# A 7x7 circular convolution by partial Fourier transform: plane operations moved behind round 15's sums, a third buffer for first sums, and another order of issuers for the last writes

## The chip, the cores and the metric

One Trainium2 chip, of which the kernel uses one core. The metric is device time in microseconds for one execution; the runs of the kernel before took 256.21, 256.63 and 630.49 us, so their median is 256.63. In the profile the engines are called PE (TensorE matmul), PEld (TensorE weight load), DVE (VectorE), ACT (ScalarE), POOL (GpSimd) and SP (SyncE, which here only issues DMAs).

## The reference

An image of 224 x 224 pixels with 96 channels, x, is convolved with 7 x 7 taps of 96 x 96 weights, w. The reference goes through a two-dimensional Fourier transform, so the convolution is circular in both directions:

```python
def reference(x, w):                       # x 1x224x224x96, w 7x7x96x96, bf16
    wp = jnp.pad(w, ((0, H - K), (0, W - K), (0, 0), (0, 0)))
    Xf = rfft2(x.astype(float32), axes=(1, 2))
    Wf = rfft2(wp.astype(float32), axes=(0, 1))
    Yf = jnp.einsum('bhwi,hwio->bhwo', Xf, Wf)
    return irfft2(Yf, s=(H, W), axes=(1, 2)).astype(bfloat16)
```

## The kernel before

**Stages.** The kernel transforms only along the rows' direction H, in blocks of 28 rows (j, 8 of them), with 17 frequencies (rounds s = 0 to 16; 0 and 16 are real, the others complex). Along W it keeps the seven taps and folds them by a two-phase scheme into three small products per frequency (m = 0, 1, 2 in the code) on differences and sums of the pixels, the planes J. W is cut into 7 tiles of 32 pixels (t = 0 to 6; the last is called TL). Each tile goes through three steps. The forward transform fills xf (matmuls with Fm). Then come 17 rounds, one for each frequency, written to a scratch buffer in HBM (tiles 0 to 5) or kept on chip (tile 6). Then comes the inverse transform (matmuls with Gm, or with GY for the last tile), which reads the scratch buffer, and whose result is written to the output. The inverse work of the tile before and the forward work of the tile after are filled in between the matmuls of a round (`mid` and `end`). Tiles 0 and 1 run four rounds apart beside each other; from tile 2 on one tile follows another.

**A round** is the function b_round (line 578). It takes two PSUM banks, b0 and b1, out of eight that are handed round in turn. A complex round does this:

- TensorE: 19 matmuls of 96x96 into b0, then the fill, then 14 into b1.
- ScalarE copies three parts of b0 into tt_ (scaled by -0.5).
- VectorE forms the first sums u (line 667) out of the rest of b0 and tt_, which releases b0. After the fill it forms v (line 675 or 678) out of b1 and tt_, which releases b1.
- The y sum, v plus u into the buffer yf (or, in the last tile, xn and xf), is ysum (line 681). It runs on VectorE where `ydve` is set and on GpSimd elsewhere, and it is the last reader of u and v.

tt_, u and v come from one pool, tv, with two buffers for each name: the third round from a given one reuses its buffers and has to wait until that round's y sum has read them.

**Plane operations.** Three rounds share one plane buffer J. The function jit (line 518) returns three VectorE operations that fill it from xf: the four differences, one sum, and two sums of differences; a real round needs only the differences. From tile 2 on they are issued in bursts, a group ahead: the dictionary plan (line 951) says in which round. The next tile's first group is issued in round 14. In a burst round all three stand behind that round's v and y sum, and GpSimd's sums that follow in a round with plane operations are made to wait for the last of them (line 697).

**Order.** Every engine executes its instructions in the order in which the code issues them; each issue is tied to the one before (helper at line 92, so nearly all rows of the profile have that line, and the tiles' names tell them apart).

**The end.** After tile 6's rounds, its y sums are transposed by VectorE, and 16 pairs of matmuls make the output of the eight blocks, two halves for each block. VectorE and ScalarE empty one half each into a buffer, and then a DMA of 168 KB writes the block: blocks 0, 2, 4 and 6 from SyncE, 1, 3 and 5 from GpSimd, 7 from ScalarE (line 1005).

Of the kernel before, what the change touches and what calls it, by code (L numbers as in the profile page):

```python
# [9 lines left out]
F32 = mybir.dt.float32  # L10
ALU = mybir.AluOpType
# [9 lines left out]
NJ = 8  # L21
# [13 lines left out]
SA = 13  # L35
# [6 lines left out]
SH2 = (0, 8, 13, 17)  # L42
FR0 = (0, 8, 17)
FR2 = ((0, 10, 24, 10), (10, 17, 34, 6))
MERGE = ()
NP2 = 0
FI = 6
LROUND = {8: 16, 11: 15}
# [10 lines left out]
def kernel(  # L59
# [7 lines left out]
    _, H, W, C = x.shape  # L67
# [504 lines left out]
    def pairs(ap):  # L572
        return ap.rearrange("p (r g o) -> p g r o", r=2, o=2)

    def yp(ap):
        return ap.rearrange("p g (r o) -> p g r o", o=2)

    def b_round(t, s, mid, end, ydve=False, planes=()):
# [25 lines left out]
                TE.matmul(o, lhsT=pl[:, (HALO - k) * NJ:(HALO - k) * NJ + 128], rhs=wv,  # L604
                          start=(k == 0 and not add), stop=(k == len(tp) - 1 and not both and m != 2 or not add and not both and k == len(tp) - 1))
        b0, b1 = bank(), bank()
        merge = t < 2 and s in MERGE
        tt_ = tv_pool.tile([128, 4 * C], F32, name="tt_")
        if s in REAL and t == TL and s == NS - 1:
            mid()  # L610
            for part in range(2):
                conv(b1, part * 2 * C, 0, part, both=True)
                for mi, m in enumerate((2, 1)):
                    conv(b1, (part * 2 + mi) * C, m, part, add=True)
            SE.copy(out=yp(ym), in_=pairs(b1[:, 0:4 * C]))
            load["a"] += 480
            end()
        elif s in REAL:
            for part in range(2):
                conv(b0, part * C, 0, part)  # L620
            if t == TL:
                SE.copy(out=tt_.rearrange("p (r m o) -> p r m o", r=2, m=2),
                        in_=b0[:, 0:2 * C].rearrange("p (r o) -> p r o", o=C).unsqueeze(2).to_broadcast([128, 2, 2, C]))
            else:
                SE.copy(out=tt_[:, 0:2 * C], in_=b0[:, 0:2 * C])
            mid()
            settle(0)
            for mi, m in enumerate((2, 1)):
                for part in range(2):
                    conv(b1, (part * 2 + mi if t == TL else mi * 2 + part) * C, m, part)  # L630
            if t == TL:
                VE.tensor_tensor(out=yp(ym), in0=pairs(tt_[:]), in1=pairs(b1[:, 0:4 * C]), op=ALU.add)
            else:
                VE.tensor_tensor(out=ym,
                                 in0=tt_[:, 0:2 * C].rearrange("p (r o) -> p r o", o=C).unsqueeze(1).to_broadcast([128, 2, 2, C]),
                                 in1=b1[:, 0:4 * C].rearrange("p (m r o) -> p m r o", m=2, r=2), op=ALU.add)
            load["a"] += 110 + 0.9 * 192
            load["v"] += 540
            for f in planes:
                f()  # L640
            settle(1)
            end()
        else:
            v = tv_pool.tile([128, 2, 2, C], F32, name="v")
            if merge:
                conv(b0, 2 * C, 0, 0, both=True)
                conv(b0, 2 * C, 2, 0, add=True)
                conv(b0, 3 * C, 1, 0, add=True)
                conv(b0, 0, 0, 1)
                conv(b0, C, 0, 2)  # L650
                SE.mul(out=tt_[:], in_=b0[:, 0:4 * C], mul=-0.5)
                u, pr = tt_[:, 2 * C:4 * C].rearrange("p (m o) -> p m o", m=2), tt_[:, 0:2 * C]
            else:
                for part in range(3):
                    conv(b0, part * C, 0, part)
                conv(b0, 3 * C, 2, 0)
                conv(b0, 4 * C, 1, 0)
                u = tv_pool.tile([128, 2, C], F32, name="u")
                if t == TL:
                    SE.mul(out=tt_[:, 0:C], in_=b0[:, 0:C], mul=-0.5)  # L660
                    SE.copy(out=tt_[:, C:3 * C], in_=b0[:, C:3 * C])
                    load["a"] += 240
                else:
                    SE.mul(out=tt_[:, 0:3 * C], in_=b0[:, 0:3 * C], mul=-0.5)
                pr = tt_[:, C:3 * C]
            if not merge:
                VE.scalar_tensor_tensor(out=u[:], in0=b0[:, 3 * C:5 * C].rearrange("p (m o) -> p m o", m=2), scalar=-0.5,
                                        in1=tt_[:, 0:C].unsqueeze(1).to_broadcast([128, 2, C]), op0=ALU.mult, op1=ALU.add)
            mid()
            settle(0)  # L670
            for mi, m in enumerate((2, 1)):
                for pi, part in enumerate((1, 2)):
                    conv(b1, (pi * 2 + mi if t == TL else mi * 2 + pi) * C, m, part)
            if t == TL:
                VE.tensor_tensor(out=v[:], in0=pr.rearrange("p (r o) -> p r o", r=2).unsqueeze(2).to_broadcast([128, 2, 2, C]),
                                 in1=b1[:, 0:4 * C].rearrange("p (r m o) -> p r m o", r=2, m=2), op=ALU.add)
            else:
                VE.scalar_tensor_tensor(out=v.rearrange("p m r o -> p m (r o)"),
                                        in0=pr.unsqueeze(1).to_broadcast([128, 2, 2 * C]), scalar=-2.0,
                                        in1=b1[:, 0:4 * C].rearrange("p (m q) -> p m q", m=2), op0=ALU.mult, op1=ALU.add)  # L680
            def ysum(eng):
                if t == TL:
                    return eng.tensor_tensor(out=yp(ym), in0=pairs(v.rearrange("p r m o -> p (r m o)")),
                                             in1=u.rearrange("p m (g o) -> p (m g) o", o=2).unsqueeze(2).to_broadcast([128, C, 2, 2]), op=ALU.add)
                return eng.tensor_tensor(out=ym, in0=v[:],
                                         in1=u.unsqueeze(2).to_broadcast([128, 2, 2, C]), op=ALU.add)
            if ydve:
                ysum(VE)
            last = None
            for f in planes:  # L690
                last = f()
            settle(1)

            def pool_sum(after):
                y = ysum(GE)
                if after is not None:
                    tc.add_manual_dep(y.ins, after.ins.name, SYNC, reason="sum after VectorE")
            if (t, s) in YLATE:
                later.append((YLATE[(t, s)], pool_sum))
            elif not ydve:  # L700
                pool_sum(last)
            load["a"] += 490 if merge else 410
            load["v"] += (560 if ydve else 250 if t < 2 else 0) + (560 if merge else 900)
            end()
        if t != TL and s == y1 - 1:
            dma(scr_tiles[t].rearrange("w j s e -> (w j) s e")[:, y0:y1], yf[:, 0:y1 - y0].rearrange("p s r m o -> p s (r m o)"))
# [132 lines left out]
    stmp_cm.__exit__(None, None, None)  # L839
    yf_pool = ctx.enter_context(tc.tile_pool(name="yf", bufs=YBUF))  # L840
    tv_pool = ctx.enter_context(tc.tile_pool(name="tv", bufs=2))
    load["v"], load["a"] = BIAS, 0.0

    t_pool = t2_pool = yo_pool = None
# [87 lines left out]
    for t in range(2, NT):  # L932
# [16 lines left out]
        for g, (s0, s1) in enumerate(JGB):  # L949
            if g + 1 < len(JGB) - (t == TL) or t + 1 < NT:  # L950
                plan[s0 if g + 1 < len(JGB) else s0 - 1] = g
        for s in range(NS):
            now = ()
            if s in plan:
                g = plan[s]
                now = jit(t, g + 1) if g + 1 < len(JGB) else jit(t + 1, 0)
            if s == 3:
                queue_c(t - 1)
            if t in (3, 4):
                next(gp, None)  # L960
            mid = fills(qs, 2 * s)
            if t == TL and s in LROUND:
                now = late_planes(LROUND[s])
            if t == TL and SA - 1 <= s < NS - 1:
                now = [lambda i=s - SA + 1: turn_a(i)]
            b_round(t, s, mid, fills(qs, 2 * s + 1), s == SA - 1 if t == TL else bool(now), now)
    turn_b()
    load["v"] = 2 * BIAS + load["a"]
    for f in cj:
# [16 lines left out]
    def second(j, h, pc, yo):  # L986
# [3 lines left out]
        yj = yo[0:MO, (j % 2) * 2 * NC:(j % 2 + 1) * 2 * NC].rearrange("p (w h q) -> p h w q", w=4, h=2)  # L990
        tail_evac(yj[:, h], pc.rearrange("p (w q) -> p w q", w=4), NC)
    order = [(j, h) for j in range(NJ) for h in range(2)]
    warm(WARM0)
    live = {k: first(*k) for k in order[:FI]}
    LF = 4
    for i, (j, h) in enumerate(order):
        if i % 4 == 0:
            yo = t_pool.tile([128, TW // 2, 2 * C], BF16, name="tt").rearrange("p w e -> p (w e)")
        second(j, h, live[(j, h)], yo)
        k = i + 8 - LF  # L1000
        if FI <= k < len(order):
            live[order[k]] = first(*order[k])
        if i % 2 == 1:
            w0 = TL * 2 * TW
            eng = SE if j == NJ - 1 else GE if j % 2 else DE
            eng.dma_start(out=out[0, j * B:(j + 1) * B, w0:w0 + 2 * TW, :].rearrange("m (q w) c -> m q (w c)", q=4), in_=yo[0:MO, (j % 2) * 2 * NC:(j % 2 + 1) * 2 * NC])
    if not NP2:
        ps0_cm.__exit__(None, None, None)
# [30 lines left out]
```

## Time and profile before

| | us |
|---|---|
| median of three runs | 256.63 |
| the profiled execution | 255.99 |
| its span, first to last instruction | 254.28 |
| TensorE busy (matmuls) | 245.4 |
| VectorE busy | 214.8 |
| ScalarE busy | 200.4 |
| GpSimd busy | 107.9 |
| VectorE u waiting for GpSimd sums (yf, xn) | 5.3 and 1.2 |
| GpSimd sum, one (yf) | 1.00 |
| VectorE u, v | 0.35, 0.54 |
| last tile's transposes end, last matmuls begin | 243.6 |

The granted TensorE clock is 0.995 over the span. A matmul's time in the profile is its way through the array; since matmuls are pipelined, the next one starts 42 ns after a 96x96 one. A wait of TensorE is therefore best read from the distance between starts. The page's slices show TensorE at nine tenths or more in all but the first and the last slices, so waits inside the span are short and are found in the chain of waits, which lists in order of time which engine held up the end, and in the timelines of single engines. Landing of a DMA means that its last part has reported to its semaphore.

### The profile page before, as it was taken

What the parts mean: (1) busy time and instruction counts of PE and PEld (TensorE: products, weight loads), DVE (VectorE), ACT (ScalarE), POOL (GpSimd) and SP (SyncE); (2) the same over time, 40 slices, a digit from 0 to 9 for tenths busy, and PEclk for the clock granted to TensorE, in tenths of its full rate; (3) what the DMA queues carried; (4) which work ended last, traced back from release to release, by engine and by line L of the source; (5) the groups of instructions that cost most, each with busy time, mean ns of one, the idle gap of its engine ahead of it and who ended that gap; (6) DMA issues with size and microseconds to landing.
All of it is one profiled execution on the core that took longest, in us unless ns stands there. A gap on an engine that the chain in (4) does not pass through costs nothing.

```text
span 254.3 us, 11853 instructions
## 1 busy us (share of the span) xinstructions
PE 245.4 (97%) x4981; PEld 230.8 (91%) x4981; DVE 214.8 (84%) x463; ACT 200.4 (79%) x499; POOL 107.9 (42%) x173
## 2 busy tenths in 40 slices
PE   8999999999999999999999999999999999999990
PEld 2789999999999999999999989999999999999970
DVE  7999899899889979789688887788978889989981
ACT  7989977584966977998988879988897976567671
POOL 7886514454457444332433324533233332465430
PEclk9999999999999999999999999999999999999998
DMA  7953103711111589997959369697969853496245
GB/s 176 260 162 97 48 5 93 233 49 49 49 52 50 187 206 143 280 318 214 304 171 256 111 184 275 194 257 180 333 214 208 246 183 105 134 170 182 60 134 163
DMA packets 41511, 42.80 MB, mean 168 GB/s; under 512 B 30836, under 2 KB 33072, under 8 KB 41458
## 3 DMA queue, kind: packets, MB, share of 16 engines
q1 hardware_dynamic: 41140, 41.36, 59.0%
q8 instruction: 39, 0.64, 1.1%
q0 software_dynamic: 192, 0.52, 0.7%
q10 hardware_dynamic: 126, 0.17, 0.2%
q14 instruction: 14, 0.11, 0.2%
HBM read 22.37 MB, written 19.66 MB: 165 GB/s over the span
## 4 chain that ended last, share of the span: by engine, by line
PE 88%; DVE 3%; issue 2%; SPq 1%; DMA 1%; POOL 1%; ACT 1%; POOLq 0%; DVEq 0%
PE pb L92 88%; SPq L92 1%; DVE WF L92 1%; DMA out_dram<-J 1%; DVE J L92 1%; DVE u L92 1%; POOL yf L92 0%; POOL xf L92 0%; DVE v L92 0%; DVE xf L92 0%; POOLq L1034 0%; ACT xf L92 0%; DVE tt L92 0%; ACT tt__7303 L92 0%; ACT tt__574 L92 0%
## 5 line engine op out<-in xcount | busy, mean ns | idle before, releaser
L92 PE MATMUL pb<-WF,J 96*128 96x96 bf16 x2782 | 160.9, 206 | 0.1
L92 PEld LDWEIGHTS <-J 96*128 96x128 bf16 x2782 | 137.0, 98 | 7.1 <-issue 0.2
L92 POOL TENSOR_TENSOR yf<-v,u 128x384 bf16<-128x384 f32 x70 | 68.9, 1000 | 118.4 <-issue 63.9
L92 ACT CAST xf<-pb 96x408 bf16<-96x408 f32 (+8 forms) x146 | 68.3, 489 | 4.2 <-PE pb L92 2.2
L92 PE MATMUL pb<-WF,xf 96*128 96x96 bf16 x991 | 62.0, 206 | 0.9 <-ACT xf L92 0.4
L92 DVE TENSOR_TENSOR J<-xf 96x1824 bf16<-96x1824 bf16 (+1 forms) x82 | 56.2, 724 | 0.1
L92 PEld LDWEIGHTS <-xf 96*128 96x128 bf16 x991 | 49.3, 98 | 1.6 <-issue 0.7
L92 PE MATMUL pb<-Fm,xn 118*128 118x136 bf16 (+5 forms) x576 | 44.4, 203 | 0.2 <-DVE u L92 0.2
L92 PE MATMUL pb<-tt,Gm 102*84 102x384 bf16 (+1 forms) x132 | 32.1, 325 | 0.0
L92 ACT CAST WF<-pb 96x480 bf16<-96x480 f32 (+1 forms) x59 | 29.2, 570 | 0.6 <-PE pb L92 0.6
L92 ACT CAST yo<-pb 84x384 bf16<-84x384 f32 (+1 forms) x65 | 27.9, 485 | 2.3 <-PE pb L92 2.3
L92 PEld LDWEIGHTS <-xn 118*128 118x128 bf16 x576 | 29.0, 97 | 0.5 <-issue 0.3
L92 ACT CAST J<-pb 84x384 bf16<-84x384 f32 (+1 forms) x65 | 28.0, 486 | 0.9 <-PE pb L92 0.9
L92 DVE TENSOR_TENSOR J<-J 96x912 bf16<-96x912 bf16 (+2 forms) x41 | 22.5, 548 | 0.0
L92 PE MATMUL pb<-wq 128*128 128x120 bf16 (+1 forms) x288 | 21.8, 226 | 0.1
L92 PEld LDWEIGHTS <-wq 128*128 128x128 bf16 x288 | 19.7, 149 | 0.6 <-ACT wq L92 0.4
L92 POOL TENSOR_TENSOR xn<-v,u 128x384 bf16<-128x384 f32 x11 | 10.0, 923 | 8.7 <-DVE J L92 5.7
L92 DVE TENSOR_TENSOR yf<-v,u 128x384 bf16<-128x384 f32 x20 | 11.3, 567 | 0.8 <-DMA scr<-yf 0.2
L92 PEld LDWEIGHTS <-Gm 102*84 102x84 bf16 (+1 forms) x132 | 11.3, 118 | 0.1
L92 ACT COPY xf<-xf 96x816 bf16<-96x816 bf16 (+4 forms) x16 | 10.0, 683 | 0.0
L92 DVE TENSOR_TENSOR WF<-WF 96x960 bf16<-96x960 bf16 x14 | 9.4, 721 | 0.1
L92 PE MATMUL pb<-wu 128*128 128x512 bf16 x24 | 7.8, 504 | 1.1 <-DVE ct L92 1.1
(409 smaller groups left out, 254.5 us busy)
## 6 DMA issues: line engine op xcount, KB each, us to landing
scr<-yf SPq DMA_DIRECT2D x30, 288.0 KB
xn<-in_x_dram SPq DMA_DIRECT2D x12, 672.0 KB
tt<-scr SPq DMA_DIRECT2D x24, 336.0 KB
out_dram<-yo SPq DMA_DIRECT2D x12, 252.0 KB
out_dram<-J SPq DMA_DIRECT2D x12, 252.0 KB
tt<-scr SPq DMA_DIRECT2D x6, 288.0 KB
scr<-yf SPq DMA_DIRECT2D x6, 192.0 KB
WF<-in_x_dram SPq DMA_DIRECT2D x2, 343.0 KB
```

The source lines that it names most:

```text
L92: r = fn(*a, **k)
```

## The change

Three things. First, of the burst that prepares the next tile's first group (issued in round 14), only the four differences stay in round 14; the other two operations go to round 15, behind its v. Round 15's y sum stays on GpSimd and follows them. Second, u gets a pool of its own with three buffers; tt_ shrinks to three parts, and the last tile's real round 0 uses a v buffer for its copy. Third, the last writes are issued by SyncE (0, 1, 3, 5), GpSimd (2, 4, 6) and ScalarE (7). A branch that no round took (merge, with MERGE empty) is deleted. On every engine the order of instructions is as before, except that at four tile boundaries VectorE has the two plane operations behind u and v of round 15 in place of ahead of them.

```diff
-            tt_ = tv_pool.tile([128, 4 * C], F32, name="tt_")
+            tt_ = tv_pool.tile([128, 3 * C], F32, name="tt_")
...
             if t == TL:
-                SE.copy(out=tt_.rearrange("p (r m o) -> p r m o", r=2, m=2),
+                v = tv_pool.tile([128, 2, 2, C], F32, name="v")
+                SE.copy(out=v[:],
...
-                u = tv_pool.tile([128, 2, C], F32, name="u")
+            u = u_pool.tile([128, 2, C], F32, name="u")
...
     tv_pool = ctx.enter_context(tc.tile_pool(name="tv", bufs=2))
+    u_pool = ctx.enter_context(tc.tile_pool(name="u", bufs=3))
...
+        carry = []
         for s in range(NS):
-            now = ()
+            now, carry = carry, []
             if s in plan:
                 g = plan[s]
                 now = jit(t, g + 1) if g + 1 < len(JGB) else jit(t + 1, 0)
+                if g + 1 == len(JGB):
+                    now, carry = now[:1], now[1:]
...
-            b_round(t, s, mid, fills(qs, 2 * s + 1), s == SA - 1 if t == TL else bool(now), now)
+            b_round(t, s, mid, fills(qs, 2 * s + 1), s == SA - 1 if t == TL else s in plan, now)
...
+    WENG = (DE, DE, GE, DE, GE, DE, GE, SE)
...
-            eng = SE if j == NJ - 1 else GE if j % 2 else DE
+            eng = WENG[j]
```

More of the change, by code (lines that the diff above doesn't have):

```diff
@@ L44 @@
 FR2 = ((0, 10, 24, 10), (10, 17, 34, 6))
-MERGE = ()
 NP2 = 0
@@ L606, in b_round @@
         b0, b1 = bank(), bank()
-        merge = t < 2 and s in MERGE
-        tt_ = tv_pool.tile([128, 4 * C], F32, name="tt_")
+        tt_ = tv_pool.tile([128, 3 * C], F32, name="tt_")
         if s in REAL and t == TL and s == NS - 1:
@@ L631, in b_round @@
             if t == TL:
-                VE.tensor_tensor(out=yp(ym), in0=pairs(tt_[:]), in1=pairs(b1[:, 0:4 * C]), op=ALU.add)
+                VE.tensor_tensor(out=yp(ym), in0=pairs(v.rearrange("p r m o -> p (r m o)")), in1=pairs(b1[:, 0:4 * C]), op=ALU.add)
             else:
@@ L644, in b_round @@
             v = tv_pool.tile([128, 2, 2, C], F32, name="v")
[L645 to L652, printed above, removed]
-            else:
[L654 to L657, printed above, removed]
-                u = tv_pool.tile([128, 2, C], F32, name="u")
[L659 to L668, printed above, removed]
+            for part in range(3):
+                conv(b0, part * C, 0, part)
+            conv(b0, 3 * C, 2, 0)
+            conv(b0, 4 * C, 1, 0)
+            u = u_pool.tile([128, 2, C], F32, name="u")
+            if t == TL:
+                SE.mul(out=tt_[:, 0:C], in_=b0[:, 0:C], mul=-0.5)
+                SE.copy(out=tt_[:, C:3 * C], in_=b0[:, C:3 * C])
+                load["a"] += 240
+            else:
+                SE.mul(out=tt_[:, 0:3 * C], in_=b0[:, 0:3 * C], mul=-0.5)
+            pr = tt_[:, C:3 * C]
+            VE.scalar_tensor_tensor(out=u[:], in0=b0[:, 3 * C:5 * C].rearrange("p (m o) -> p m o", m=2), scalar=-0.5,
+                                    in1=tt_[:, 0:C].unsqueeze(1).to_broadcast([128, 2, C]), op0=ALU.mult, op1=ALU.add)
             mid()
@@ L701, in b_round @@
                 pool_sum(last)
-            load["a"] += 490 if merge else 410
-            load["v"] += (560 if ydve else 250 if t < 2 else 0) + (560 if merge else 900)
+            load["a"] += 410
+            load["v"] += (560 if ydve else 250 if t < 2 else 0) + 900
             end()
```

## The prediction

> **What bounds the kernel now.** The page's first part comes first, then the chain of waits in order of time, because a chain that is nearly all one engine shows by its few interruptions what can be won.
>
> ```profile
> PE 245.4 (97%) x4981; PEld 230.8 (91%) x4981; DVE 214.8 (84%) x463; ACT 200.4 (79%) x499; POOL 107.9 (42%) x173
> ```
>
> TensorE is busy 97% of 254.3 us. Busy could hide slow feeding, so I also took the distance between the starts of neighbouring matmuls: for 96x96 it is 42 ns in nearly all of 3765 cases, and all distances beyond the usual one of their shape add up to 6.3 us, 2.9 us of it in the first 30 us and 0.6 us in the last 12 us. Between lies what this change can win on TensorE. The chain in order of time (start, duration, what) names the places:
>
> ```profile
> 63.14 1.94 issue
> 65.08 1.02 POOL yf L92
> 66.10 0.02 issue
> 66.12 0.37 DVE u L92
> 66.49 0.04 issue
> 66.53 53.22 PE pb L92 x1186
> 119.75 0.04 DVEq L92
> 119.79 0.05 DVE u L92
> 119.83 0.04 issue
> 119.88 23.93 PE pb L92 x482
> ...
> 151.13 0.21 DVE u L92
> 151.33 0.04 issue
> 151.38 87.59 PE pb L92 x1778
> ```
>
> Three times in the middle TensorE waits for VectorE's u, the operation that empties bank b0 of a round. At 66 u itself waited for a GpSimd sum. At 119.8 and 151.3 the timeline of VectorE shows what stood ahead of u (last column: what ended an idle time, none here):
>
> ```profile
> 117.84 1.32 DVE L92 TENSOR_TENSOR J<-xf 96x1824 bf16<-96x1824 bf16 x2
> 119.09 0.47 DVE L92 TENSOR_TENSOR J<-J 96x608 bf16<-96x608 bf16 x1
> 119.47 0.35 DVE L92 SCALAR_TENSOR_TENSOR u<-pb,tt__3633 128x192 f32<-128x192 f32 x1
> 119.74 0.54 DVE L92 SCALAR_TENSOR_TENSOR v<-tt__3633,pb 128x384 f32<-128x384 f32 x1
> ```
>
> These are round 14's three plane operations (1.10, 0.31 and 0.47 us; the first line holds two) and round 15's u and v. ScalarE had u's other input ready at 118.05. The end is another stage:
>
> ```profile
> 244.69 4.42 SPq L92 DMA_DIRECT2D out_dram<-tt  x4
> 245.75 0.88 POOL L92 DMA_DIRECT2D out_dram<-tt  x1 [3.22 <-DVE tt L92]
> 246.85 0.59 POOL L92 DMA_DIRECT2D out_dram<-tt  x1 [0.23 <-issue]
> 248.15 0.59 POOL L92 DMA_DIRECT2D out_dram<-tt  x1 [0.70 <-ACT tt L92]
> 248.74 1.44 ACTq L92 DMA_DIRECT2D out_dram<-tt  x1
> ```
>
> The eight last writes are issued here. By the trace's landing records write 6 (SyncE) is complete at 253.02 and write 7 (ScalarE) at 253.19; then only the closing barrier runs.
>
> **Plane operations behind round 15's sums.** Four boundaries (tiles 2 to 5) move the 0.31 and 0.47 us operations from before u to behind v. Nothing is added; VectorE's work between round 14's y sum and round 16's stays the same. At 119.5 u can start when the first plane operation lets it, 117.84 + 1.02 = 118.86 in place of 119.47, and ends at 119.2. TensorE was ready at 119.57 (42 ns after its last start, 119.53) and started at 119.88, so this wait of 0.30 us goes. At 150.87 the same step brings u's end from 151.32 to 150.71, TensorE was ready at 150.91 and started at 151.38: 0.46 us go, and with v also 0.6 us earlier the 0.13 us that TensorE waits at 151.67 for v's bank. The boundaries at 182 and 214 show no TensorE wait, so they win nothing. Sum: 0.89 us.
>
> What the moved operations may delay: round 16's y sum follows them at 120.3 in place of 120.2, and its bank is next written by round 1, after 121.6. Round 15's GpSimd sum now has to wait for the last of them: v ends near 119.6, the operations near 120.3, and the sum started at 120.42 before, so it moves by nothing. The planes themselves are read in round 1 of the next tile (from 121.17), 0.9 us after they are done. All of that is costed at nothing; a slip of more than 0.9 us would uncover it.
>
> **Third buffer for u.** u of a round no longer waits for the GpSimd sum two rounds back but for the one three back; v keeps two buffers and takes over the wait for two back, which u held for it until now. So v can never wait longer than u did. VectorE waited so 15 times (5.3 us for yf, 1.2 us for the last tile's xn), but only at 66 did TensorE wait behind it: u starts at 65.68 (v's end) in place of 66.12 and ends at 66.04, ahead of TensorE's readiness at 66.22, so 0.31 us go. ScalarE is packed there (64.1 to 68), so it is what is late next; bounds 0 and 0.31, and I take 0.31 because no TensorE wait on ScalarE appears between 40 and 240.
>
> In the last tile the four waits of 0.31 us are on VectorE's own chain, which sets the end (u at 240.74, v, a GpSimd sum, the transposes). One would count 4 x 0.27 = 1.1 us there. The trace says no: a plane operation that starts while GpSimd sums is stretched. The 96x1824 one takes 1.10 us as a rule and 1.39 us at 62.70 and at 50.71, where GpSimd's sum ran 0.43 us into it; with 0.12 us of overlap (220.83, 225.51) it still takes 1.10. So it ends no earlier than the sum's end plus 0.97. In the last tile each of these operations already starts 0.11 to 0.12 us before a sum ends (225.51 against 225.63), and u coming 0.3 us earlier only makes it start that much deeper into the sum. I take 0; the other bound is 0.27, since v at 230.11 waits for TensorE and only the one wait after it (233.3) could carry to the end.
>
> The ScalarE copy of the last tile's round 0 goes into a v buffer, waiting for round 14's VectorE sum and an earlier GpSimd sum, both over 2 us old by then: nothing.
>
> **Last writes.** The halves of write k are ready at 244.66, 245.16, 245.81, 246.47, 247.13, 247.79, 248.28 and 248.66. SyncE issues 0.03 us after readiness and takes 0.80 to 0.93; GpSimd starts 0.36 to 0.59 after and takes 0.59 to 0.88. So write 1 goes out on SyncE at 245.65 when write 0's issue is over (was 245.75), 2 on GpSimd near 246.3 (245.84), 3 on SyncE at 246.5 (246.85), 4 on GpSimd near 247.5 (247.16), 5 on SyncE at 247.82 (248.15), 6 on GpSimd near 248.65 (248.31), 7 on ScalarE at 248.74 as before. From issue to landing the eight took 2.82, 2.87, 3.25, 3.57, 3.58, 4.15, 4.71 and 4.45 us: it grows with what is under way, not with the engine. Write 6 would land at 252.8 (4.15) to 253.35 (4.7). Write 7's issue took 1.44 us while SyncE and GpSimd issued beside it; SyncE is idle then after the change, so it costs between 0.8 and 1.44, and it lands between 252.6 and 253.2. The end moves from 253.19 to between 252.6 and 253.35: a win of 0.6 to a loss of 0.16. I take a win of 0.2, the middle.
>
> Sum: 0.89 + 0.31 + 0 + 0.2 = 1.4 us. The profiled execution took 255.99 (span 254.28 and 1.71 around it), so 254.6 on its scale. The two near runs are 256.21 and 256.63, and the stated median, 256.63, is 0.64 above the profiled one; the mean of the three, 256.28, less 1.4 gives 254.9.
>
> **Rivals.** *GpSimd is the worse issuer for the end.* For: it starts 0.36 us after readiness where SyncE takes 0.03, and write 6, next to last, now pays that. Against: GpSimd's landings lie on one line with SyncE's. Priced by the 0.3 us later issue alone: the 0.2 us become a loss of 0.2, total 1.0, 255.3. The Trainium skill, in DMA: Bandwidth & Descriptors, Latency and other measured facts, gives about 1 us to the first byte of a GpSimd DMA and 0.6 us for SyncE or ScalarE; by that estimate write 6 alone loses 0.4 us. Its section Issuing engines are not separate DMA queues adds that spreading issues over engines saves only issue time, since all run on the same 16 DMA engines; by that alone the end term is nothing and the total 1.2 us.
>
> *The waits come back elsewhere.* TensorE meets a bank that ScalarE empties late, at 66 and after the boundaries, as ScalarE is 79% busy. Then only the wait at 150.9 is won: 0.4 to 0.6 us, 255.8. Against it speaks that after 66 no TensorE wait other than these appears in 170 us.
>
> *Slower: the planes are late for round 1.* If the moved operations slip by over 0.9 us (their first in-queue chance is behind v, which needs TensorE's b1 and now GpSimd's sum), the next tile's first round stalls, four times. Past that point each 0.1 us costs 0.4; a slip of 1.4 us costs 2.0, less 1.4 won: 256.9. Against: v starts at 119.1 to 119.2 there and GpSimd is idle before it (3.14 us).
>
> *VectorE's relief counts too and the writes win their best*: 0.89 + 0.31 + 0.27 + 0.6 = 2.1, 254.2. *The change does nothing* because v takes over every wait: it would hold for the third buffer alone, and the boundary order is plain in the program, so it is only part of the second rival.
>
> **How the numbers follow.** Chances: forecast 0.52, GpSimd 0.18, waits back 0.16, slower 0.06, best 0.08. Predicted 254.9. The lower end takes in the best case on the profiled run's scale (255.99 - 2.1 = 253.9), the upper end a win of nothing on the median's (256.6); only the slower case is out, so the range 253.9 to 256.6 leaves under 2 in 10. Two per cent, 5.1 us, is about what a measurement of this kernel can tell from no change; every case lies inside: faster 0.02, same 0.95, slower 0.03, the tails for what I did not see.
>
> **What would show it.** In the changed profile no TensorE wait on u near 66, 119 and 151, u of round 15 right behind the first plane operation, v with the GpSimd waits, last landing at 252.6 to 253.4 less 1.2, and the 96x1824 operations of the last tile longer than 1.10 us. Wrong would be: new TensorE waits after 66 or in round 1, VectorE's transposes ending over 1.5 us earlier than before (243.6), or write 6 landing alone at the end.

## The result and the profile after

| | before | after |
|---|---|---|
| median (7 runs each) | 256.42 us | 255.59 us |
| range | 256.06 to 256.63, and one execution of 630.49 | 255.14 to 255.85 |
| ratio, 95% interval | | 0.9961, 0.9948 to 0.9974 |
| profiled execution | 255.99 | 255.59 |
| its span | 254.28 | 253.87 |
| last transpose ends, last write landed | 243.60, 253.19 | 243.11, 252.79 |

The change makes the kernel 0.8 us faster by the medians (0.3%) and 1.0 us by the ratio (0.4%), where 1.4 us were forecast. The spans differ by only 0.41 us, for two reasons that have nothing to do with the change. The two executions did not start alike: the matmul at 16 us, which no part of the change reaches, comes 0.21 us later in the execution after. And TensorE pauses there for 0.22 us at 173 us. Such differences of the first 16 us were 0 to 0.77 us among the executions below, with the profiled one of before the luckiest. So I compare the two traces matmul by matmul: both kernels have the same 4981 matmuls in the same order, and each step in the difference of their starts is a wait that came or went. A negative number is a wait that is gone.

| place (us in the trace before) | step, us | what it is |
|---|---|---|
| 60.5 | +0.11 | new wait for VectorE's weight difference WF |
| 66.5 | -0.32 | u near 66 us, which waited for a GpSimd sum |
| 119.9 | -0.30 | u of round 15 |
| 151.4 and 151.8 | -0.46 and -0.13 | u, then v of round 15 |
| 156.9 | +0.07 | new wait for a bank that ScalarE empties |
| 173 | +0.22 | pause without a cause in the trace; in this execution alone |
| 242.5 | +0.18 | longer wait of the first matmul with GY for the transposes |

The first part of the page, once more with TensorE at 97%, shows nothing of this:

```profile
PE 245.1 (97%) x4981; PEld 230.5 (91%) x4981; DVE 216.6 (85%) x463; ACT 200.3 (79%) x499; POOL 108.9 (43%) x173
```

The chain of waits does (start, duration, what; start and end of its part after 60 us):

```profile
60.71 0.00 issue
60.72 111.77 PE pb L91 x2364
172.49 0.06 issue
172.54 66.35 PE pb L91 x1352
...
242.57 0.55 DVE xf L91
243.12 0.04 issue
243.16 3.96 PE pb L91 x36
```

The chain no longer leaves TensorE for u at 66, 119.8 and 151.3: it stays there from 60.72 to 238.9 but for a 0.06 us step at 172.5. At the end it is on VectorE, as before. VectorE's timeline at the first boundary (start, duration, operation, in brackets what ended an idle time, none here) shows the new order:

```profile
117.75 1.09 DVE L91 TENSOR_TENSOR J<-xf 96x1824 bf16<-96x1824 bf16 x1
118.77 0.35 DVE L91 SCALAR_TENSOR_TENSOR u<-pb,tt__3634 128x192 f32<-128x192 f32 x1
119.03 0.54 DVE L91 SCALAR_TENSOR_TENSOR v<-tt__3634,pb 128x384 f32<-128x384 f32 x1
119.50 0.30 DVE L91 TENSOR_TENSOR J<-xf 96x304 bf16<-96x304 bf16 x1
119.72 0.46 DVE L91 TENSOR_TENSOR J<-J 96x608 bf16<-96x608 bf16 x1
120.11 0.54 DVE L91 TENSOR_TENSOR yf<-tt__3684,pb 128x384 bf16<-128x384 f32 x1
```

u starts at 118.77, right behind the first plane operation, and the other two follow v and are done by 120.2, before round 1 reads them.

The last writes (start of the issue, its duration; four of SyncE in one line):

```profile
244.20 3.93 SPq L91 DMA_DIRECT2D out_dram<-tt  x4
245.78 0.88 POOL L91 DMA_DIRECT2D out_dram<-tt  x1 [3.75 <-DVE tt L91]
247.02 0.59 POOL L91 DMA_DIRECT2D out_dram<-tt  x1 [0.36 <-ACT tt L91]
248.25 1.44 ACTq L91 DMA_DIRECT2D out_dram<-tt  x1
248.32 0.58 POOL L91 DMA_DIRECT2D out_dram<-tt  x1 [0.70 <-DVE tt L91]
```

ScalarE's issue takes 1.44 us as before, though SyncE is now done at 248.13 and idle. By the landing records write 7 lands last, at 252.79, and GpSimd's write 6 at 252.42.

### The profile page after: what moved, and what is told of

The parts are those of the page before. It is cut to its first block, busy times and chain, and to the rows that moved or that the text cites. A ratio compares the mean times of both kernels' runs of the same rounds, so it can differ in the third digit from the quotient of the medians.

```text
span 253.9 us, 11837 instructions
## 1 busy us (share of the span) xinstructions
PE 245.1 (97%) x4981; PEld 230.5 (91%) x4981; DVE 216.6 (85%) x463; ACT 200.3 (79%) x499; POOL 108.9 (43%) x173
## 4 chain that ended last, share of the span: by engine, by line
PE 91%; DVE 3%; ACT 2%; issue 1%; POOL 0%; POOLq 0%; DVEq 0%
PE pb L91 91%; ACT WF L91 1%; DVE WF L91 1%; ACT xf L91 1%; DVE J L91 1%; DVE v L91 1%; DVE u L91 0%; POOL xf L91 0%; DVE xf L91 0%; POOLq L1028 0%; DVE tt L91 0%; ACT tt__577 L91 0%; DVE wu L91 0%; DVE ct L91 0%; DVEq L91 0%
## 5 line engine op out<-in xcount | busy, mean ns | idle before, releaser
L91 POOL TENSOR_TENSOR yf<-v,u 128x384 bf16<-128x384 f32 x70 | 69.6, 1009 | 117.2 <-DVE v L91 61.2
```

The lines of the kernel that those rows point to most:

```text
L91: r = fn(*a, **k)
```

## The experiments

All ratios are to the kernel before, run on the same chip in the same session; a median of before stands beside them. "Shift to 239" is the step of the matmul starts between 40 and 239 us, against the profiled execution before, which leaves the unlike starts out. "GY wait" is how much later than usual the second matmul with GY starts (0.24 us before).

**The moved plane operations alone.** The kernel before, with the edit of jit's results only:

```diff
+        carry = []
...
-            now = ()
+            now, carry = carry, []
...
+                if g + 1 == len(JGB):
+                    now, carry = now[:1], now[1:]
...
```

> The kernel before with the moved plane operations alone. If the boundary waits are the main win (the forecast): TensorE's waits at 119.5 (0.30 us), 150.9 (0.46) and 151.7 (0.13) are gone, the one at 66.2 (0.31) stays, and the time falls by 0.5 to 0.9 us (ratio about 0.997). If the waits only come back elsewhere: new TensorE waits of the same size within a tile after each boundary, and a time within 0.3 us of the kernel before. If the planes come late: TensorE waits in round 1 of tiles 3 to 6, and a longer time.

Median 255.86 (before 256.71), ratio 0.998, 0.9955 to 1.0004; of itself the ratio leaves open whether there is a gain. The trace does not: shift to 239 is -0.79, in the steps -0.30, -0.46, -0.13 and +0.07 of the table. The wait at 66 stays; here in the chain, u and TensorE behind it:

```profile
66.92 0.37 DVE u L92
67.29 0.04 issue
67.34 171.62 PE pb L92 x3593
```

**The third buffer alone**, with the smaller tt_ that makes room for it; order of the plane operations and issuers as before:

```diff
-        tt_ = tv_pool.tile([128, 4 * C], F32, name="tt_")
+        tt_ = tv_pool.tile([128, 3 * C], F32, name="tt_")
...
-                u = tv_pool.tile([128, 2, C], F32, name="u")
+            u = u_pool.tile([128, 2, C], F32, name="u")
...
```

> The kernel before with the three-part tt_ and three buffers for u alone. If u's wait on GpSimd is what TensorE waited for at 66: that wait (0.31 us) is gone and the time falls by 0.1 to 0.3 us; the waits at 119.5 and 150.9 stay. If an early u only leads the next two-input VectorE operation into a GpSimd sum: the weight difference near 59 takes 1.4 to 1.5 us in place of 1.17, the 608-element operations of the last tile 0.70 in place of 0.466, TensorE's wait at 60.5 grows by 0.1, and of the 0.3 us only 0.2 is left. If the relief in the last tile counts after all: the transposes end over 0.6 us earlier.

Median 256.60, ratio 0.9994, 0.9986 to 1.0003. Shift to 239 is -0.24 (the steps at 60.5 and 66.5), and the GY wait rises to 0.43, which gives 0.19 back: 0.05 us remain. Of the three cases the second came: the weight difference takes 1.49 us, the 96x608 operations of the last tile 0.70. The chain shows the waits that this part leaves alone, and none at 66:

```profile
61.06 58.92 PE pb L91 x1299
119.98 0.04 DVEq L91
120.01 0.05 DVE u L91
...
151.35 0.21 DVE u L91
151.56 0.04 issue
151.60 88.19 PE pb L91 x1788
```

**The issuers alone.**

```diff
+    WENG = (DE, DE, GE, DE, GE, DE, GE, SE)
...
-            eng = SE if j == NJ - 1 else GE if j % 2 else DE
+            eng = WENG[j]
```

> The kernel before with the new issuers of the last writes alone. If the order of issuers is worth something (the forecast's 0.2 us): from the first write's readiness to the last landing 8.3 us in place of 8.53. If it is worth nothing, because the last issue is the same 1.44 us one on ScalarE: 8.5 to 8.65 us, and the time within 0.15 us of the kernel before. If GpSimd is the worse issuer: write 6 lands last and the stretch takes 8.7 us or more.

Median 256.70, ratio 0.9998, 0.9989 to 1.0006. From the first write's readiness to the last landing it takes 8.76 us; with the old issuers 8.53 (before) and 8.90 twice (the two runs above). That is none of the three cases: the stretch is longer than the profiled one before, yet write 7 lands last and not write 6, and the profiled one before turns out to be the shortest of three. A gain, if there is one, is too small for these times to show.

**The changed kernel again**, in the same session, unaltered.

> The changed kernel, unchanged. If the TensorE wait of 0.22 us at 172.3 without a semaphore, the one of 0.07 at 155.7, the VectorE pause of 0.29 us at 234.6 and the 0.21 us lost before 16 belong to that execution alone, they are absent or elsewhere here and the span is up to 0.5 us shorter (253.4); if they belong to the program, they come again at the same places and the span is 253.9.

Median 255.75, ratio 0.9965, 0.9953 to 0.9976. Shift to 239 is -1.06. The pause at 173 is absent; the new waits at 60.5 and 156.9 and the GY wait (0.42) recur. The parts add up to about that: 0.79 and 0.24.

**Write 7 on SyncE instead of ScalarE.**

```diff
-    WENG = (DE, DE, GE, DE, GE, DE, GE, SE)
+    WENG = (DE, DE, GE, DE, GE, DE, GE, DE)
```

> The changed kernel with write 7 issued by SyncE instead of ScalarE; all else as changed. In the changed kernel write 7 was ready at 248.17, ScalarE's issue of it took 1.44 us, and it landed last at 252.79, 0.37 us behind write 6. Theory: the long issue holds the end. SyncE takes 0.80 for the same write, so write 7's issue ends 0.64 us sooner, its landing comes 0.3 to 0.6 us sooner, and the time from the first write's readiness to the last landing falls from 8.6 to 8.7 to 8.2 to 8.4; ratio to the kernel before near 0.995, against 0.9961 of the change. Rival: the landings go one behind the other at the pace of the transfers, the backlog sets the end; then the issue takes 0.80 but the last landing does not move by over 0.1 us, and the ratio stays at 0.996 to 0.997.

Median 255.66 (before 256.58), ratio 0.9964, 0.9951 to 0.9978. The five issues of SyncE now are

```profile
244.06 4.84 SPq L91 DMA_DIRECT2D out_dram<-tt  x5
```

and write 7's takes 0.80 us where ScalarE took 1.44. Yet it lands at 252.60, 8.57 us after the first readiness, against 8.51 to 8.76 with ScalarE. The rival holds: the long issue costs nothing that these runs show.

**Moved operations and these issuers, u with two buffers.** The first experiment's kernel with the last writes of the one just told.

> The kernel before with the moved plane operations and with the new issuers, write 7 on SyncE; u keeps two buffers in the old pool. Theory: the third buffer's 0.2 us on TensorE are given back in the last tile (first GY matmul waits 0.42 us with it, 0.23 without), so leaving it out costs nothing: the same ratio as the three parts together with write 7 on SyncE, within 0.0008, TensorE 0.79 us earlier by 239 us (wait of 0.33 at 66.9 stays) and the first GY matmul's wait 0.22 to 0.24. Rival: the third buffer is worth its 0.24 us or more; then this one is 0.001 or more slower than that kernel.

Median 255.68, ratio 0.9966, 0.9953 to 0.9978: the same time without the third buffer as with it. At 239 us TensorE is 0.30 us behind the other kernel, but the GY wait is 0.22 and not 0.42, so at the end 0.09 us are left of it. The theory holds: what the third buffer wins near 66 us is given back in the last tile.

**The sums of the last tile left out.**

```diff
-                y = ysum(GE)
+                y = GE.memset(ym, 0.0) if t == TL else ysum(GE)
```

> The changed kernel, with the last tile's GpSimd y sums left out: a memset of the same output stands in the place of each sum (so those y values are not computed), with its waits on VectorE unchanged. Theory: a plane operation with two inputs in SBUF is held while a GpSimd operation reads SBUF; a memset reads none. So the 96x608 operations at 228.2 and 233.3 fall from 0.70 to about 0.47 us and the 96x1824 ones that begin inside a sum back to 1.10, u and v follow that much earlier. If VectorE's pause of 0.29 us between u and v near 234.6 comes from the same cause it goes too and the first GY matmul's wait falls from 0.42 to about 0.2. Rival: the operations are long because of their own waits or of TensorE; then they stay at 0.70 with the memset in place of the sum. If the pause stays, it is not GpSimd's reading that makes it.

One execution, 255.29 us. The 96x608 operations fall from 0.71 and 0.70 to 0.47 and 0.46 us, VectorE's pause is gone, and the first matmuls with GY run without a wait at all. But a memset reads neither u nor v and does not wait for them, so the memsets do not lie where the sums lay. It shows that the sums lengthen these operations, and little more. What kind of neighbour does it is seen at another place of the same trace: VectorE's own y sum, also with two inputs in SBUF, takes 0.56 us at 235.18 with memsets beside it all the time, and 0.66 at 235.90 in the kernel before, where a GpSimd sum runs 0.24 us into it.

**All writes from SyncE.**

```diff
+    WENG = (DE,) * 8
```

> The changed kernel with all eight last writes issued by SyncE. From issues of 0.93, 0.88 and then 0.80 us one behind the other, write 7 goes out near 250.0 on the changed profile's time, 1.8 us later than before. Theory: the transfers' backlog sets the end, and the issue only feeds it; with the 2.8 us that the first two writes take from issue to landing write 7 lands at 252.8 or up to 0.6 later, so the time from the first readiness to the last landing is 8.6 to 9.3 us (8.6 to 8.75 with the change). Rival: each write takes the 4.5 us that the last ones take now, counted from its own issue; then it lands at 254.5 and that time is 10.3.

```profile
244.41 7.37 SPq L91 DMA_DIRECT2D out_dram<-tt  x8
```

One execution, 256.32 us. The issues follow each other every 0.91 us at the end, and each write lands 2.76 to 2.88 us after its issue began, the last 9.38 us after the first readiness: just past the theory's 9.3, far from the rival's 10.3. Here every write lands equally soon after its own issue, so it is the issues, one behind the other, that set the end. With three issuers the writes go out faster, and the time to land grows from 2.8 to 4.5 us. The stretches of the changed kernel's end (the last two columns: busy share of the DMA engines, GB/s) show why the issuer of write 7 no longer matters:

```profile
246.00:248.00 2.00, 1.61 (x17) 1.31 (x15) 1.80 (x4) 1.64 (x4) 1.26 (x2) 1.00 0.69 191
248.00:250.00 2.00, 0.00 (x0) 0.00 (x0) 0.17 (x1) 0.17 (x1) 0.58 (x1) 1.00 0.80 237
250.00:252.00 2.00, 0.00 (x0) 0.00 (x0) 0.00 (x0) 0.00 (x0) 0.00 (x0) 1.00 0.75 230
```

From 248 on the transfers run at 230 to 237 GB/s, while nearly nothing is issued any more.

**Two buffers for u in the last tile only**, first attempt:

```diff
-            u = u_pool.tile([128, 2, C], F32, name="u")
+            if t == TL and len(ul) < 2:
+                ul.append(u_pool.tile([128, 2, C], F32, name="u"))
+            u = ul[s % len(ul)] if t == TL else u_pool.tile([128, 2, C], F32, name="u")
...
+    ul = []
```

> The changed kernel, but in the last tile u alternates between two of its three buffers, so that there u waits for the GpSimd sum of two rounds back again; elsewhere it keeps three. Theory: the third buffer wins 0.21 us before 70 us and loses 0.18 at the end, where u starts earlier, the plane operations then start deeper inside the GpSimd sums, and VectorE pauses 0.29 us before v near 234.6. With two buffers there the 96x608 operations at 228 and 233 fall back to 0.47 us, the pause goes, the first GY matmul's wait falls from 0.42 to 0.22 to 0.24, and the kernel is 0.2 us faster than the changed one: ratio to the kernel before near 0.9955. Rival: the wait comes from something else that the change moved; then it stays at 0.42 and the ratio at 0.9962.

Median 256.20 (before 256.76), ratio 0.9978, 0.9970 to 0.9987: a smaller gain than the change's (ratios 0.9960 to 0.9965 in other sessions), and the GY wait is 0.87. The edit is at fault: with one buffer in the list at round 1, rounds 1 and 2 share it. VectorE's timeline there:

```profile
217.13 0.34 DVE L91 SCALAR_TENSOR_TENSOR u<-pb,tt__6600 128x192 f32<-128x192 f32 x1
217.40 0.54 DVE L91 TENSOR_TENSOR v<-tt__6600,pb 128x384 f32<-128x384 f32 x1
218.98 0.36 DVE L91 SCALAR_TENSOR_TENSOR u<-pb,tt__6650 128x192 f32<-128x192 f32 x1 [1.04 <-POOL xn L91]
```

u waits 1.04 us for the sum of the round just before. The miss teaches something: VectorE is so full in the last tile that 0.65 us of that delay, at 219 us, still stand in the GY wait at 242 us (0.87 instead of 0.22). So a delay of VectorE here does reach the end, as the change's 0.18 us do.

**One sum left out**, that of round 11 of the last tile:

```diff
+                y = GE.memset(ym, 0.0) if (t, s) == (TL, 11) else ysum(GE)
```

> The changed kernel, with a memset of the same output in the place of one GpSimd sum, that of round 11 of the last tile (so those y values are not computed); all other sums stay. Theory: VectorE's pause of 0.29 us between u and v near 234.6 is made by this sum, which starts during u; without it v follows u at once, the first GY matmul's wait falls from 0.42 to 0.1 or less, while the 96x608 operations at 228.2 and 233.3 stay at 0.70, since the sums beside them are still there. Rival: the pause is made by the place in the program or by the longer operations before it; then it stays at 0.28 to 0.29.

One execution, 255.72 us. The theory falls: the pause is there without the sum that lay over it, and so is the GY wait of 0.43.

```profile
234.45 0.34 DVE L91 SCALAR_TENSOR_TENSOR u<-pb,tt__7153 128x192 f32<-128x192 f32 x1
235.08 0.56 DVE L91 TENSOR_TENSOR v<-tt__7153,pb 128x384 f32<-128x384 f32 x1 [0.28 <-POOL xn L91]
```

The profile names GpSimd as what ended this idle time, and means the memset, which ended 0.07 us before. But v needs the sum of round 10, which ended 1.0 us before u did; in the changed kernel the same 0.29 us stand as "issue".

**Two buffers in the last tile, strictly alternating, and the changed kernel beside it.**

```diff
-            u = u_pool.tile([128, 2, C], F32, name="u")
+            while t == TL and len(ul) < 2:
+                ul.append(u_pool.tile([128, 2, C], F32, name="u"))
+            u = ul[s % 2] if t == TL else u_pool.tile([128, 2, C], F32, name="u")
...
+    ul = []
```

> The changed kernel, with u in the last tile alternating strictly between two buffers. In the run before this one of that purpose rounds 1 and 2 shared one buffer, so u of round 2 waited for the GpSimd sum of round 1 (u at 218.98, v before it at 217.40), and VectorE stayed 0.65 us late to the end: first GY matmul's wait 0.87. Here each wait is that of the kernel before, two rounds back. Theory (the third buffer's gain is given back in the last tile by deeper overlap with the sums and by VectorE's pause): first GY matmul's wait 0.22 to 0.24, no pause near 234.6, 96x608 operations at 0.47, 0.2 us faster than the changed kernel, ratio near 0.9955. Rival: VectorE's last stretch has no slack against TensorE, so that with TensorE 1.1 us earlier than in the kernel before it is VectorE that sets the end in any case: then the wait is 0.4 or more, and the ratio no better than 0.996.

> The changed kernel again, on the chip of the two-buffer run, for the comparison of the two: ratio 0.996, first GY matmul's wait 0.42 to 0.43, VectorE's pause of 0.28 to 0.29 us, write 7 last to land. Theory of the give-back: 0.2 us slower than the two-buffer kernel. Rival: the same.

Medians 255.26 (254.98 to 255.58) and 255.68 (255.52 to 255.75), before 256.72; ratios 0.9944, 0.9931 to 0.9958, and 0.9960, 0.9948 to 0.9973. The two-buffer kernel is the faster one, though the intervals of the ratios overlap a little. VectorE's timelines, first the two-buffer kernel, then the changed one:

```profile
233.58 0.84 DVE L91 TENSOR_TENSOR xf<-xf 96x608 bf16<-96x608 bf16 x3
234.34 0.35 DVE L91 SCALAR_TENSOR_TENSOR u<-pb,tt__7144 128x192 f32<-128x192 f32 x1
234.61 0.54 DVE L91 TENSOR_TENSOR v<-tt__7144,pb 128x384 f32<-128x384 f32 x1
235.18 0.65 DVE L91 TENSOR_TENSOR xn<-v,u 128x384 bf16<-128x384 f32 x1
```

```profile
233.49 1.08 DVE L91 TENSOR_TENSOR xf<-xf 96x608 bf16<-96x608 bf16 x3
234.49 0.34 DVE L91 SCALAR_TENSOR_TENSOR u<-pb,tt__7153 128x192 f32<-128x192 f32 x1
235.10 0.56 DVE L91 TENSOR_TENSOR v<-tt__7153,pb 128x384 f32<-128x384 f32 x1 [0.27 <-issue]
235.69 0.56 DVE L91 TENSOR_TENSOR xn<-v,u 128x384 bf16<-128x384 f32 x1
```

The three plane operations take 0.84 us against 1.08, and v follows u at once. TensorE starts its first matmuls with GY in both, and then waits in one of them (start, duration, in brackets the idle time ahead):

```profile
241.36 1.41 PE L91 MATMUL pb<-xf,GY 128*112 128x384 bf16 x6
```

```profile
241.58 0.33 PE L91 MATMUL pb<-xf,GY 128*112 128x384 bf16 x1
242.15 1.03 PE L91 MATMUL pb<-xf,GY 128*112 128x384 bf16 x5 [0.25 <-DVE xf L91]
```

By the matmul starts the GY wait is 0.22 and 0.41, so 0.19 of the 0.42 us between the medians belong to the mechanism, and the rival, by which VectorE sets the end in any case, falls. Another 0.22 us between the two profiled executions lie ahead of 160 us, before the last tile, where the programs differ in nothing.

## Why the prediction was right, and where its sum was off

The time came out inside the range and within 2%, for most of the reasons given; the gain was 0.83 us by the medians (0.96 and 1.04 in the two repeats) and not 1.4. Of the 0.69 us between 254.9 and 255.59, 0.14 are the start value (256.28 against the later median 256.42) and the rest is the sum. The range was wide enough to hold a change that does nothing, so the time alone would speak for no mechanism; the steps of the matmul starts do. The intervals here reach less than 0.3% to either side, so a gain of 0.4% can be told from none, where the prediction put that limit at 2%.

**Plane operations behind round 15's sums, 0.89.** Right in each of its three terms (0.30, 0.46, 0.13 predicted; 0.30, 0.46, 0.13 measured, and again in every kernel with this part). Nothing slipped: round 16's y sum starts at 120.11 and round 1 meets no new wait, so the rival "slower: the planes are late" falls. One cost was not seen: 0.07 us at 156.9, a bank that ScalarE empties late, which is the rival "the waits come back elsewhere" at a small scale (0.36 us in all with the 0.11 and 0.18 below, against 1.21 us of waits that went). Net 0.82.

**Third buffer for u, 0.31 and 0.** This is the step that failed. The 0.31 at 66 is right (0.32), with v taking the GpSimd wait at 66.34. But u comes earlier at 58.90 too, and then the weight difference WF starts deep inside a GpSimd sum: 59.18 to 60.66, 1.48 us, where it took 1.17 before and 0.64 undisturbed. TensorE waits 0.11 us longer for it. The rows before and after, GpSimd's two sums in one line:

```profile
57.98 1.95 POOL L92 TENSOR_TENSOR yf<-v,u 128x384 bf16<-128x384 f32 x2 [1.95 <-issue]
59.28 1.17 DVE L92 TENSOR_TENSOR WF<-WF 96x960 bf16<-96x960 bf16 x1
```

```profile
58.19 1.96 POOL L91 TENSOR_TENSOR yf<-v,u 128x384 bf16<-128x384 f32 x2 [1.95 <-issue]
59.18 1.48 DVE L91 TENSOR_TENSOR WF<-WF 96x960 bf16<-96x960 bf16 x1
```

The prediction used this very stretching for the last tile and did not look for it before. The Trainium skill, in SBUF — State Buffer, Who interferes with whom, says that a VectorE instruction with two SBUF inputs contends with a GpSimd instruction that reads SBUF, and not with one that only writes it. The traces agree with both halves: 1.48 us for 0.64 inside a sum here, and 0.56 us beside memsets for the y sum at 235.18 in the run with memsets, the same as undisturbed.

In the last tile the argument for nothing was half right. Its sign, 96x1824 operations longer than 1.10 us, did not come: three of the four still take 1.10, at 220.10, 224.77 and 229.83, since they start no deeper in a sum than before. The one at 215.33 takes 1.25, but 1.24 in the kernel with the moved operations alone too. It is the two 96x608 operations that start deeper in a sum and stretch (0.70 for 0.47 us), so they gain little. What the argument missed is VectorE's pause of 0.29 us ahead of v. In the profile before there is none:

```profile
234.30 0.84 DVE L92 TENSOR_TENSOR xf<-xf 96x608 bf16<-96x608 bf16 x3
235.06 0.35 DVE L92 SCALAR_TENSOR_TENSOR u<-pb,tt__7149 128x192 f32<-128x192 f32 x1
235.33 0.54 DVE L92 TENSOR_TENSOR v<-tt__7149,pb 128x384 f32<-128x384 f32 x1
235.90 0.66 DVE L92 TENSOR_TENSOR xn<-v,u 128x384 bf16<-128x384 f32 x1
```

Compare the changed kernel's lines in the last experiment, where the matmuls run 0.48 us earlier than in these. With that taken off, the plane operations start 0.33 us earlier than before and u 0.09 us, so the stretch has taken most of the third buffer's gain. v starts 0.25 us later, and the y sum behind it ends only 0.17 us later, since no GpSimd sum stretches it now (0.56 for 0.66). By the same 0.17 us TensorE's wait for the transposes grows there (0.41 for 0.24; 0.18 in the profile after), outside the bounds of 0 and 0.27 and on the side of a loss, so the rival "VectorE's relief counts too" falls. Without the pause v would have begun 0.08 us before u's end, as elsewhere, at 234.55 in the changed profile and so 0.37 us earlier; that this alone would have made a gain of the loss is argued and not shown. A net of 0.03 was left of the third buffer: 0.32 less 0.11 and 0.18.

What makes the pause stays open. It is no wait of the program that the trace shows: u was done, TensorE's sums and ScalarE's copy were there. It stood in all seven executions of kernels with three buffers in the last tile, 0.27 to 0.29 us long, apart from the one with memsets throughout, and in no other. In those kernels this v is the 576th of VectorE's instructions in the trace, waits included; in the ones without a pause it is the 569th or the 592nd. In all seven a transfer of 8 KB on an instruction queue starts 0.64 to 0.67 us after v starts; in the other kernels that transfer lies elsewhere (231.4 to 232.9 or 237.1 to 237.8). That points to the place in VectorE's instruction stream rather than to the sums, but no run moved the instruction and nothing else, and the longer plane operations ahead of it were there in all seven too.

**Last writes, 0.2.** Not settled. From first readiness to last landing the eight executions with these issuers took 8.63 us on average (8.51 to 8.76), the three with the old ones 8.78 (8.53 to 8.90). That is a gain of 0.15 by the means, but the ranges overlap, and the run with the issuers alone has a ratio whose interval includes none (0.9989 to 1.0006). The reason for the better end of its bounds was wrong: ScalarE's issue did not shrink with SyncE idle (1.43 to 1.44 in every run), and by the run with write 7 on SyncE a shorter one would have won nothing. The rival "GpSimd is the worse issuer" falls: write 6 lands 0.3 to 0.4 us ahead of write 7. The Trainium skill's rule in DMA: Bandwidth & Descriptors, Issuing engines are not separate DMA queues, that several issuers save only issue time, fits both runs: one issuer for all loses 0.75 us, and which engine issued write 7 made no difference. The figure of 1 us to the first byte of a GpSimd DMA, in the section Latency and other measured facts of the same page of the Trainium skill, was not measured by any run, and it did not make write 6 the last to land.

The measured terms give 0.82 + 0.03 = 0.85, or 1.00 with 0.15 for the writes. Both lie among the gains of the three sessions, 0.83 to 1.04, so these do not decide on the writes either.

## What to carry to other kernels

Two kernels with the same matmul order are best compared start by start: steps of 0.1 us show that no ratio can. A buffer that lets one engine start earlier pays only where the next engine in line can use it, and where it moves an operation into contention it can take the gain back, so give it to the stage that waits and not to all. Once transfers are still under way long after the last issue, a shorter last issue wins nothing; all issues from one engine, one behind the other, did cost time.

## What the runs showed of the hardware

- A VectorE operation with two SBUF inputs that starts inside a GpSimd sum grew by what was left of that sum, less about 0.13 us: 0.47 to 0.70 with 0.37 us left, 0.64 to 1.48 with 0.97 left. With 0.12 us left it did not grow, and beside memsets neither. Where the two started within 0.02 us of each other, near 82 us, it went either way: VectorE's grew from 0.78 to 1.63 us in the profile before, the sum from 1.00 to 1.66 in the one after.
- For the same 168 KB write the issue takes 0.80 to 0.99 us on SyncE, 0.58 to 0.60 on GpSimd (0.88 for its first) and 1.43 to 1.44 on ScalarE, here with the other engines issuing beside it or not.
- The first 16 us, which hold the same work in all these programs, differed by up to 0.77 us between executions, nearly as much as the whole gain; in three executions of the changed kernel they differed by 0.53.
